# Word loads behind k and v, the first q from another queue, and three steps swapped in the opening of a fused attention and feed-forward kernel

## The chip, the cores and the metric

The kernel runs on one core of one Trainium2 chip. The metric is the device time of one execution in microseconds; three runs of the kernel before took 885.45, 887.29 and 890.8 us, so their median is 887.29 us. Engines are named as the profile names them: PE is TensorE's matmul, PEld its weight load, DVE is VectorE, ACT is ScalarE, POOL is GpSimd, SP is SyncE, which here only starts DMAs.

## The reference

```python
kv  = einsum('bhsd,bhse->bhde', k, v)         # q, k, v: 8 batches, 8 heads, 576 rows, 64 columns, float32
o   = einsum('bhsd,bhde->bhse', q, kv)
x   = o / sqrt(mean(o*o, axis=-1) + 1e-6) * g_norm
x   = x.transpose(0, 2, 1, 3).reshape(4608, 512)
h   = x @ w_in                                # w_in 512 x 2048, w_out 2048 x 512, both float64
out = (h * tanh(softplus(h))) @ w_out         # 4608 x 512, float32
```

The weights arrive as float64. The kernel takes them as pairs of 32-bit words and joins each pair into one float32 number itself.

## The kernel before

The work has two parts. Part 1 goes over nine tiles of 512 tokens. Each tile needs attention's output x, which takes the tile's q and the matrix kv of its batch (or of two batches, since 512 tokens don't divide 576); x is then multiplied by `w_in`, and the activated product g goes to DRAM. Part 2 reads g and multiplies by `w_out`. Both large products are done as two-by-two block products with seven multiplications instead of eight (Strassen's scheme in Winograd's form, `PROD`), and each float32 operand is split into a rounded part and a remainder (`split`, L121 and L122), so that one product is three matmuls.

The opening, with which the change deals, prepares three things at once:

- The eight weight blocks of `w_in` (`conv[0]` to `conv[7]`). A block's steps are LOAD (two DMAs of 512 KB, L137), SCALE (ACT, L142), JOIN (three DVE operations, L147 to L149), DIFF (three DVE operations, L157 to L159), and BLOCKS and SUMS (splits by ACT and DVE). A block's raw words are kept in a room that an earlier block may still hold: blocks 0, 4 and 7 share the tile `w64`, blocks 2 and 5 the tile `wf6`, blocks 3 and 6 the tile `wf7`; block 1 uses `wf5`. A LOAD into a room waits until JOIN of the earlier block has read it.
- k and v. Batch 0's are loaded by `kv_first` (L226) in two halves and multiplied by `kv_first_product` (L234, 72 small matmuls for each half); `kv_keep` (L269) copies the result out of PSUM. For batch 1 the heads go by pairs, p = 0 to 3: `k_load(1, p)` starts four DMAs (L213 and L214, tiles km, kr, vm, vr), `k_product(1, p)` multiplies (L252). Two sets of these tiles exist, so the load of p = 2 waits for the product of p = 0.
- q. The first tile's q comes in four chunks by `rows_load` (L295), each 128 tokens by 8 heads by 64 numbers. TensorE transposes them (step `transpose`, L325: four transposes for each pair of heads; unit 0 takes heads 0 to 3, unit 1 heads 4 to 7), `turned` copies them out of PSUM (ACT for unit 0, L338; DVE for unit 1, L336), `project` multiplies by kv (L360), `square`, `sums`, `rstd` (logarithm L408, exponential L409) and `normalize` (L430) give x.

Every engine works through its instructions in the order in which the code is written. In the opening that order stands in the code directly; from the first product on, `at(t, f)` puts a step behind the product of slot t, and within a slot steps run in the order of the `at` calls. Slot 0 holds the first product (L527), and seven slots make one round.

All DMAs before part 2 are started by SP (its queue is q1 in the profile), but for the stores of the last tile, which ACT starts (queue q10). Each DMA signals one of eight semaphores, which are handed out in turn to the DMAs of SP and ACT together; an instruction that starts a DMA waits until the DMA that had its semaphore before has landed. The order of instructions below writes them DMAHW0 to DMAHW7.

Of the kernel before, what the change touches and what calls it, by code (L numbers as in the profile page):

```python
# [27 lines left out]
def linear_attention_rms_mish_ffn(  # L28
# [34 lines left out]
    nc = tc.nc  # L63
    B, H, S, D = q.shape
# [3 lines left out]
    P = 128  # L68
# [37 lines left out]
    gcol = const.tile([P, 1], F32, name="gcol")  # L106
# [121 lines left out]
    def kv_first_product(n):  # L228
        kt, vt = kv0
        for hp in range(n.start, n.stop):  # L230
            for c in range(9):
                for o in range(2):
                    r, d = slice(o * D, (o + 1) * D), slice(c * D, (c + 1) * D)
                    nc.tensor.matmul(kvps[r, 0, hp, :], kt[r, hp, d], vt[r, hp, d], start=(c == 0), stop=(c == 8))  # L234
# [31 lines left out]
    def kv_keep(b, n):  # L266
        for r in (slice(0, D), slice(D, P)):
            if b < T32:
                nc.scalar.copy(kvf[b][r, n, r], kvps[r, b % 2, n, :])  # L269
        if b < T32 - 1:  # L270
            return
        t = kvt[b % 2]
        for r in (slice(0, D), slice(D, P)):
            nc.scalar.copy(t[r, 0, n, r], kvps[r, b % 2, n, :])
        for r in (slice(0, D), slice(D, P)):
            nc.vector.tensor_sub(t[r, 1, n, r], kvps[r, b % 2, n, :], t[r, 0, n, r].bitcast(F32))


    def segments(j):

        n = (S - T) * j
        segs = []
        if n:
            segs.append((j - 1, S - n, slice(0, n)))
        if n < T:
            segs.append((j, 0, slice(n, T)))
        return segs

    def rows_load(j, c):
        for b, s0, cols in segments(j):  # L290
            t0, t1 = max(cols.start, c * P), min(cols.stop, (c + 1) * P)
            if t0 < t1:
                src = q[b, 0:1, s0 + t0 - cols.start:s0 + t0 - cols.start + 1, :]
                src = bass.AP(src.tensor, src.offset, [[D, t1 - t0], [S * D, H], [1, D]])
                nc.sync.dma_start(rows[j][t0 - c * P:t1 - c * P, c, :].rearrange("p (h d) -> p h d", d=D), src)  # L295

    rows = {}
    qs, ss = {}, {}
# [145 lines left out]
    def x_form(f):  # L444

        a11, a12, a21, a22 = block(0, 0), block(1, 0), block(0, 1), block(1, 1)
        if f == S1:
            nc.vector.tensor_add(xs1, a21, a22)
            nc.vector.tensor_sub(a21, a11, a21)
        elif f == S2:  # L450
            nc.vector.tensor_sub(a11, xs1, a11)  # L451
        elif f == S4:
            nc.vector.tensor_sub(a12, a12, a11)
        if f not in xforms:
            if f == A22:
                xforms[f] = fq.tile([P, 2, 2, TH], F32R, name="a22")
            else:
                pair = {A11: (A11, S1), S2: (S2, A12), S4: (S4, S3)}[f]
                t = fp.tile([P, 2, 2, 2, TH], F32R, name="gf")
                for n, g in enumerate(pair):  # L460
                    xforms[g] = t[:, n]
        t = xforms[f]
        split(t[:, 0], t[:, 1], {A11: a11, S1: xs1, S2: a11, A12: a12, S4: a12, S3: a21, A22: a22}[f])
# [7 lines left out]
    def at(t, f):  # L471
        plan.setdefault(t, []).append(f)
# [86 lines left out]
    def do(j, u, *steps):  # L559
        for s in steps:  # L560
            units[j][u][s]()
# [11 lines left out]
    LOAD, SCALE, JOIN, DIFF, BLOCKS, SUMS, STORE = range(7)  # L573

    def weights(j, *steps):
        for s in steps:
            conv[j][s]()
# [12 lines left out]
    t = wfp.tile([P, 3, 2 * T], F32, name="wf2")  # L590
    rows[0], turned_q = t[:, 0:2].rearrange("p a (c n) -> p (a c) n", c=TR // 2), t[:, 2].rearrange("p (a t) -> p a t", a=2)
    for c in range(TR):
        rows_load(0, c)
    kv0 += [wfp.tile([P, NKC, 9 * D], F32, name=f"wf{n}") for n in (3, 4)]
    kv_first(first)
    weights(1, LOAD)
    kv_first(second)
    for r in (slice(0, D), slice(D, P)):
        nc.sync.dma_start(gcol[r, :], g_norm.rearrange("(p o) -> p o", o=1))
    weights(2, LOAD)  # L600
    weights(4, LOAD)
    weights(3, LOAD)
    make_identity(nc, ident)
    kv_tiles()
# [11 lines left out]
    do(0, 1, "transpose")  # L616
    weights(0, BLOCKS)
    do(0, 0, "turned")
    weights(0, SUMS)
    do(0, 1, "turned")  # L620
    weights(1, SCALE, JOIN)
    kv_first_product(first)
    kv_keep(0, first)
    do(0, 0, "project", "square")
    weights(1, DIFF, BLOCKS)
    kv_first_product(second)
# [6 lines left out]
    k_load(1, 1)  # L633
    rows[1] = att.tile([P, TR, H * D], F32, name="qs")
    for c in range(TR):
        rows_load(1, c)
    do(0, 1, "square", "sums")
    weights(2, SCALE)
    do(0, 0, "normalize")
# [2 lines left out]
    do(0, 1, "rstd", "normalize")  # L642
    x_form(S1)
    weights(2, DIFF)
    weights(5, LOAD)


# [3 lines left out]
    for j in range(3, NF2):  # L651
        t = 3 * (j - 3) + 1
        if j < 5:
            at(t, lambda j=j: weights((6, 7)[j - 3], LOAD))
        for s, n in ((SCALE, 0), (JOIN, 0), (DIFF, 1), (BLOCKS, 1), (SUMS, 2)):
            at(t + n, lambda j=j, s=s: weights(j, s))

# [6 lines left out]
    for b in range(2, B):  # L664
        t = NS * (b - 2)
# [164 lines left out]
    for i in range(NT):  # L830
        for n in range(NQ):
            st = {"i": i, "n": n, "bank": bank_new}
            t = NS * i + 7 * n
# [3 lines left out]
    t = NS * NT  # L837
# [115 lines left out]
```

## Time and profile before

| | |
|---|---|
| three runs, us | 885.45, 887.29, 890.8 (median 887.29) |
| profiled execution, us | 885.97 |
| its span, us | 884.2 |
| PE busy | 828.1 us, 94% of the span |
| DVE busy | 608.7 us, 69% |
| ACT busy | 464.6 us, 53% |
| granted TensorE clock, mean | 0.987 of full speed |

The span runs from the first instruction to the last; the time of the execution is 1.8 us longer. All moments below are microseconds from the span's start. TensorE is nearly always busy, except in the opening: in the page's forty slices of 22 us its busy share is 4, 6 and 5 tenths in the first three, and 8 tenths or more from the fourth to the last but one. In the rows of a timeline the engine, the line and the operation are followed by the tiles (written and read), how many instructions are merged in the row, and in brackets how long the engine was idle before them and what ended that.

### The profile page before, as it was taken

What the parts mean: (1) busy time and instruction counts of PE and PEld (TensorE: products, weight loads), DVE (VectorE), ACT (ScalarE), POOL (GpSimd) and SP (SyncE); (2) the same over time, 40 slices, a digit from 0 to 9 for tenths busy, and PEclk for the clock granted to TensorE, in tenths of its full rate; (3) what the DMA queues carried; (4) which work ended last, traced back from release to release, by engine and by line L of the source; (5) the groups of instructions that cost most, each with busy time, mean ns of one, the idle gap of its engine ahead of it and who ended that gap; (6) DMA issues with size and microseconds to landing.
All of it is one profiled execution on the core that took longest, in us unless ns stands there. A gap on an engine that the chain in (4) does not pass through costs nothing.

```text
span 884.2 us, 17156 instructions
## 1 busy us (share of the span) xinstructions
PE 828.1 (94%) x7036; PEld 795.7 (90%) x7036; DVE 608.7 (69%) x804; ACT 464.6 (53%) x703; POOL 4.8 (1%) x23
## 2 busy tenths in 40 slices
PE   4658998998999999999999899999999999999997
PEld 3447898998999999999999789999999999999997
DVE  5869675886777676787764368867777677776772
ACT  3647666556675765666664444344444434434431
POOL 2000000000000000000000000000000000000000
PEclk9969999999999999999999999999999999999999
DMA  9936787987978696767477993344434443334421
GB/s 294 247 114 197 200 274 246 278 263 226 296 219 278 218 304 199 220 204 227 151 227 249 425 416 125 122 150 152 148 121 133 130 120 120 119 120 141 153 65 48
DMA packets 161038, 175.52 MB, mean 199 GB/s; under 512 B 24704, under 2 KB 142464, under 8 KB 159936
## 3 DMA queue, kind: packets, MB, share of 16 engines
q1 hardware_dynamic: 158208, 170.23, 61.8%
q10 hardware_dynamic: 2752, 4.20, 1.3%
q8 instruction: 55, 0.90, 0.4%
q14 instruction: 23, 0.19, 0.1%
HBM read 112.39 MB, written 62.00 MB: 197 GB/s over the span
## 4 chain that ended last, share of the span: by engine, by line
PE 63%; DMA 11%; DVE 10%; ACT 9%; issue 4%; SPq 2%; ACTq 0%; DVEq 0%
PE a L772 22%; PE bc L772 16%; PE a L527 13%; PE bc L527 7%; DMA gd<-ula 5%; PE s L252 2%; DMA vm<-in_v_dram 2%; DVE ur L548 1%; DMA wod<-wst 1%; ACT L412 1%; ACT gf L121 1%; DMA rd<-fl 1%; DVE gf L122 1%; DVE fa L122 1%; ACT L118 1%
## 5 line engine op out<-in xcount | busy, mean ns | idle before, releaser
L772 PE MATMUL a<-wf,gf 128*128 128x256 f32 x1632 | 201.8, 283 | 0.5 <-DVE ur L812 0.5
L772 PEld LDWEIGHTS a<-wf,gf 128*128 128x128 f32 x1632 | 198.4, 192 | 0.7 <-DVE ur L812 0.7
L122 DVE TENSOR_TENSOR gf<-g,gf 128x1024 fp32r<-128x1024 f32 (+1 forms) x123 | 132.9, 1087 | 90.7 <-ACT gf L121 90.7
L527 PE MATMUL a<-gf,wf 128*128 128x256 f32 x1296 | 173.0, 287 | 11.5 <-DVE gf L430 4.5
L527 PEld LDWEIGHTS a<-gf,wf 128*128 128x128 f32 x1296 | 162.9, 193 | 18.1 <-ACT ur L504 6.6
L527 PE MATMUL bc<-gf,wf 128*128 128x256 f32 x1296 | 170.3, 285 | 3.5 <-ACT ur L495 2.4
L527 PEld LDWEIGHTS bc<-gf,wf 128*128 128x128 f32 x1296 | 161.4, 191 | 5.1 <-ACT ur L495 2.6
L121 ACT CAST gf<-g 128x1024 fp32r<-128x1024 f32 (+1 forms) x123 | 114.6, 939 | 93.3 <-DVE g L752 65.1
L772 PE MATMUL bc<-wf,gf 128*128 128x256 f32 x1224 | 152.7, 283 | 1.0 <-DVE gf L122 1.0
L772 PEld LDWEIGHTS bc<-wf,gf 128*128 128x128 f32 x1224 | 149.4, 192 | 1.4 <-ACT gf L121 0.7
L527 PE MATMUL a<-a,wf 128*128 128x256 f32 x432 | 59.8, 289 | 2.5 <-DVE ur L548 2.5
L527 PEld LDWEIGHTS a<-a,wf 128*128 128x128 f32 x432 | 55.8, 195 | 5.6 <-DVE ur L548 3.1
L118 ACT ACTIVATE ur<-ur 128x1024 f32<-128x1024 f32 x36 | 38.1, 1059 | 37.1 <-DVE ur L548 37.1
L122 DVE TENSOR_TENSOR fa<-fl,fh 128x1024 fp32r<-128x1024 f32 x28 | 34.3, 1224 | 22.1 <-ACT fh L121 21.2
L504 ACT COPY ur<-a 128x512 f32<-128x512 f32 (+1 forms) x53 | 27.3, 516 | 37.6 <-PE a L772 24.6
L122 DVE TENSOR_TENSOR gf<-gf 128x512 fp32r<-128x512 f32 x45 | 30.4, 689 | 24.0 <-ACT gf L121 24.0
L121 ACT CAST gf<-a 128x1024 fp32r<-128x1024 f32 x17 | 17.9, 1052 | 53.5 <-DVE a L749 50.9
L121 ACT CAST gf<-gf 128x512 fp32r<-128x512 f32 x45 | 27.1, 618 | 31.4 <-DVE gf L451 19.1
L495 ACT COPY ur<-bc 128x512 f32<-128x512 f32 (+1 forms) x53 | 27.4, 517 | 29.9 <-PE bc L772 23.0
L548 DVE TENSOR_TENSOR ula<-bc,ula 128x512 f32<-128x512 f32 x36 | 24.8, 688 | 25.4 <-PE bc L527 25.3
L118 ACT ACTIVATE ula<-ula 128x512 f32<-128x512 f32 x36 | 22.8, 633 | 22.1 <-DVE ula L548 22.1
L252 PE MATMUL s<-vm,km 128*64 128x64 f32 x448 | 20.1, 235 | 14.1 <-DMA vm<-in_v_dram 14.1
(137 smaller groups left out, 858.1 us busy)
## 6 DMA issues: line engine op xcount, KB each, us to landing
g<-gd SPq DMA_DIRECT2D x18, 2048.0 KB, 8.9
gd<-ur SPq DMA_DIRECT2D x32, 512.0 KB, 4.0
wod<-wst SPq DMA_DIRECT2D x16, 896.0 KB, 5.6
wf<-wod SPq DMA_DIRECT2D x8, 1792.0 KB, 16.2
gd<-ula SPq DMA_DIRECT2D x32, 256.0 KB, 5.1
gd<-ulb SPq DMA_DIRECT2D x32, 256.0 KB, 4.3
w<-in_moe_w_out_dram SPq DMA_DIRECT2D x32, 256.0 KB, 4.6
km<-in_k_dram SPq DMA_DIRECT2D x28, 256.0 KB, 4.8
```

The source lines that it names most:

```text
L118: nc.scalar.activation(o, i, AF.Mish)
L121: nc.scalar.copy(hi, src)
L122: nc.vector.tensor_sub(lo, src, hi.bitcast(F32))
L252: nc.tensor.matmul(kvps[o * D:(o + 1) * D, b % 2, h0 // 2 + i, :], kt, vt, start=(c == 0), stop=(c == CM))
L412: nc.scalar.preload_act_table_set("natural_log_exp_and_others")
L495: then(t + 2, lambda: nc.scalar.copy(dst(st, "22"), st["c"]))
L504: then(t + 4, lambda: nc.scalar.copy(dst(st, "12"), st["a"]))
L527: nc.tensor.matmul(bank[:, jj], w[:, right, a, kc, :], xf[:, b, kc, :], start=first and jj == kc == s == 0, stop=(kc == 1 and s == 2), ski ...
L548: nc.vector.tensor_add(o, bank, o)
L772: nc.tensor.matmul(bank, gf[:, a, c, :], wo[c][:, right, b, :], start=first and c == s == 0, stop=(c == NF2 - 1 and s == 2), skip_group_ch ...
```

## The change

Four things are moved; nothing is computed in another way.

1. The first tile's q is started by ACT instead of SP (`rows_load` takes the engine as an argument; the second tile's q stays on SP).
2. The two DMAs of `g_norm` are started by GpSimd instead of SP, ahead of its memsets.
3. Block 4's LOAD goes from its place ahead of block 3's to the end of the opening, ahead of block 5's. The LOADs of blocks 6 and 7 go from slots 1 and 4 to slots 3 and 6.
4. In the opening, unit 1's `turned` goes ahead of block 0's SUMS, and block 1's SCALE and JOIN go behind the first `kv_first_product` and `kv_keep`. This is a swap of three steps.

```diff
-    def rows_load(j, c):
+    def rows_load(eng, j, c):
...
-                nc.sync.dma_start(rows[j][t0 - c * P:t1 - c * P, c, :].rearrange("p (h d) -> p h d", d=D), src)
+                eng.dma_start(rows[j][t0 - c * P:t1 - c * P, c, :].rearrange("p (h d) -> p h d", d=D), src)
...
-        rows_load(0, c)
+        rows_load(nc.scalar, 0, c)
...
-        nc.sync.dma_start(gcol[r, :], g_norm.rearrange("(p o) -> p o", o=1))
+        nc.gpsimd.dma_start(gcol[r, :], g_norm.rearrange("(p o) -> p o", o=1))
     weights(2, LOAD)
-    weights(4, LOAD)
     weights(3, LOAD)
...
     do(0, 0, "turned")
+    do(0, 1, "turned")
     weights(0, SUMS)
-    do(0, 1, "turned")
-    weights(1, SCALE, JOIN)
     kv_first_product(first)
     kv_keep(0, first)
+    weights(1, SCALE, JOIN)
     do(0, 0, "project", "square")
...
-        rows_load(1, c)
+        rows_load(nc.sync, 1, c)
...
     weights(2, DIFF)
+    weights(4, LOAD)
     weights(5, LOAD)
...
-            at(t, lambda j=j: weights((6, 7)[j - 3], LOAD))
+            at(t + 2, lambda j=j: weights((6, 7)[j - 3], LOAD))
```

Where the instructions stand shows at three places. The first is ACT's beginning. Before, its first rows are these (w is block 0's words, the tile wf that L142 reads is block 1's words, the tiles x and s are in PSUM):

```order
L588 ACT_TABLE_LOAD
L142 ACTIVATE fl<-w_136 128x1024
L121 CAST wf_217<-fl 128x256
L121 CAST wf_217<-fl 128x2x256
L338 COPY fh<-x_198 128x1024
L121 CAST wf_217<-wd 128x4x256
L142 ACTIVATE fl<-wf_148 128x1024
L269 COPY kvf_168<-s_123 64x2x64 x2
L370 ACTIVATE fa<-x_271 128x1024
```

With the change they are these:

```order
L588 ACT_TABLE_LOAD
L295 DMA wf_139<-in_q_dram 128x8x64 x4
L142 ACTIVATE fl<-w_136 128x1024
L121 CAST wf_214<-fl 128x256
L121 CAST wf_214<-fl 128x2x256
L338 COPY fh<-x_195 128x1024
L121 CAST wf_214<-wd 128x4x256
L269 COPY kvf_165<-s_123 64x2x64 x2
L142 ACTIVATE fl<-wf_148 128x1024
L370 ACTIVATE fa<-x_268 128x1024
```

The four q DMAs stand ahead of ACT's first scale, and the copies of kv stand ahead of block 1's scale instead of behind it.

The second place is SP's beginning with the change, with what each start waits for (w_136, wf_148, wf_155 and wf_158 are the words of blocks 0, 1, 2 and 3; wf_144 and wf_145 are batch 0's k and v). The four q chunks hold the semaphores DMAHW1, 3, 5 and 7:

```order
L137 DMA w_136<-in_moe_w_in_dram 128x4x256 x2
L226 DMA wf_144<-in_k_dram 128x2x576
L226 DMA wf_145<-in_v_dram 128x2x576
L137 DMA wf_148<-in_moe_w_in_dram 128x4x256 [waits DMAHW0_49]
L137 DMA wf_148<-in_moe_w_in_dram 128x4x256 [waits DMAHW1_49]
L226 DMA wf_144<-in_k_dram 128x2x576 [waits DMAHW2_49]
L226 DMA wf_145<-in_v_dram 128x2x576 [waits DMAHW3_49]
L137 DMA wf_155<-in_moe_w_in_dram 128x4x256 [waits DMAHW4_49]
L137 DMA wf_155<-in_moe_w_in_dram 128x4x256 [waits DMAHW5_49]
L137 DMA wf_158<-in_moe_w_in_dram 128x4x256 [waits DMAHW6_49]
L137 DMA wf_158<-in_moe_w_in_dram 128x4x256 [waits DMAHW7_49]
```

The q DMAs, which stood between block 0's words and k, are gone from SP; the second halves of blocks 1 and 2 and the second v now wait for a chunk of q that ACT has started.

The third place is SP around the second tile's q (qs) and the third quarter of batch 1's k and v (km to vr). Before (wf_387 is block 5, wf_441 block 6):

```order
L295 DMA qs<-in_q_dram 128x8x64 x3
L137 DMA wf_387<-in_moe_w_in_dram 128x4x256 x2
L137 DMA wf_441<-in_moe_w_in_dram 128x4x256 x2
L213 DMA km<-in_k_dram 128x2x256
L214 DMA kr<-in_k_dram 64x2x64
L213 DMA vm<-in_v_dram 128x2x256
L214 DMA vr<-in_v_dram 64x2x64
```

With the change (w_384 is block 4, wf_387 block 5, wf_522 block 6; the four rows of the fourth quarter are left out):

```order
L295 DMA qs<-in_q_dram 128x8x64 x3
L137 DMA w_384<-in_moe_w_in_dram 128x4x256 x2
L137 DMA wf_387<-in_moe_w_in_dram 128x4x256 x2
L213 DMA km<-in_k_dram 128x2x256
L214 DMA kr<-in_k_dram 64x2x64
L213 DMA vm<-in_v_dram 128x2x256
L214 DMA vr<-in_v_dram 64x2x64
...
L137 DMA wf_522<-in_moe_w_in_dram 128x4x256 x2
```

Block 6's words have gone behind two quarters of k and v, and block 4's words have come in ahead of block 5's. TensorE's order is the same in both kernels.

## Rows read from the trace of the kernel before

**Rows 1.** Stages: us, busy PE, PEld, DVE, ACT, POOL, clock, DMA share, GB/s.
```profile
0.00:7.50 7.50, 0.00 (x0) 0.00 (x0) 0.00 (x1) 2.40 (x2) 4.76 (x23) 1.00 0.84 210
7.50:14.30 6.80, 4.43 (x16) 3.18 (x16) 5.62 (x8) 2.88 (x4) 0.00 (x0) 1.00 1.17 311
14.30:20.00 5.70, 3.44 (x75) 2.89 (x76) 3.92 (x5) 1.53 (x4) 0.00 (x0) 1.00 1.06 358
...
54.60:57.00 2.40, 2.38 (x24) 2.17 (x25) 0.00 (x0) 0.00 (x0) 0.00 (x0) 0.50 0.32 78
...
72.00:90.00 18.00, 18.00 (x142) 14.73 (x141) 16.21 (x22) 12.18 (x17) 0.00 (x0) 0.91 0.52 163
```

**Rows 2.** SP's longest wait (total, times, longest), then timeline: start, us, engine, line.
```profile
SPq L137 <- DVE fl L149: 20.8, 2, 11.0
...
35.19 12.57 SPq L137 DMA_DIRECT2D wf<-in_moe_w_in_dram  x4
...
37.52 0.48 PE L252 MATMUL s<-vr,kr 64*64 64x64 f32 x4
...
47.86 0.45 SPq L213 DMA_DIRECT2D km<-in_k_dram  x1
...
54.62 1.12 PE L252 MATMUL s<-vm,km 128*64 128x64 f32 x16 [12.88 <-DMA vm<-in_v_dram]
```

**Rows 3.** Timeline, 50 to 72 us: ACT and DVE around TensorE's wait.
```profile
50.31 1.04 ACT L121 CAST wf<-wd 128x1024 fp32r<-128x1024 f32 x1
...
51.73 1.22 DVE L122 TENSOR_TENSOR wf<-wd,wf 128x1024 fp32r<-128x1024 f32 x1
...
59.05 0.58 ACT L504 COPY ur<-a 128x512 f32<-128x512 f32 x1 [7.70 <-PE a L527]
59.53 1.12 ACT L142 ACTIVATE fl<-w 128x1024 f32<-128x1024 f32 x1
...
60.69 0.69 DVE L147 TENSOR_SCALAR fl<-fl 128x1024 uint32<-128x1024 uint32 x1 [7.74 <-ACT fl L142]
...
71.75 1.22 PE L325 MATMUL x<-ident,qs 128*128 128x128 f32 x8 [2.54 <-ACT gf L378]
```

**Rows 4.** Timeline, 1 to 25 us: the opening.
```profile
1.79 5.30 SPq L295 DMA_DIRECT2D wf<-in_q_dram  x4
...
10.99 1.33 PE L325 MATMUL x<-ident,wf 128*128 128x128 f32 x5 [0.60 <-DMA wf<-in_q_dram]
...
12.11 1.91 PE L325 MATMUL a<-ident,wf 128*128 128x128 f32 x8
...
14.35 2.39 PE L234 MATMUL s<-wf,wf 64*64 64x64 f32 x72 [0.32 <-DMA wf<-in_v_dram]
...
17.32 1.12 ACT L142 ACTIVATE fl<-wf 128x1024 f32<-128x1024 f32 x1 [3.01 <-DMA wf<-in_moe_w_in_dram]
18.34 0.51 ACT L269 COPY kvf<-s 64x128 f32<-64x128 f32 x2
18.47 0.69 DVE L147 TENSOR_SCALAR fl<-fl 128x1024 uint32<-128x1024 uint32 x1 [1.71 <-ACT fl L142]
...
20.46 1.22 DVE L149 SCALAR_TENSOR_TENSOR fl<-wf,fl 128x1024 uint32<-128x1024 uint32 x1
...
22.90 0.42 DVE L159 TENSOR_TENSOR wd<-fl,wd 128x256 f32<-128x256 f32 x1
...
23.75 1.05 ACT L121 CAST wf<-wd 128x1024 fp32r<-128x1024 f32 x1
...
24.82 1.27 ACT L408 ACTIVATE fa<-bc,eps 128x512 f32<-128x512 f32 x2
```

**Rows 5.** DMA queues (packets, MB, share), first 5 to 10, then 490 to 498 us.
```profile
q1 hardware_dynamic: 4219, 1.17, 135.2%
...
q1 hardware_dynamic: 247, 3.11, 91.3%
q10 hardware_dynamic: 247, 0.25, 9.0%
```

## The prediction

> **What bounds the kernel now.** I read the stages first, then the instructions in order of time of the two stretches in which TensorE stands, then the DMA queues. From 72 us on TensorE is busy without a gap: 18.00 of 18.00 us in the stage from 72 to 90 [rows 1]. So the change, which touches only the beginning, can win or lose only what it does to the moment at which TensorE enters that stage, and everything behind it is carried along by the same number of microseconds. Ahead of it stands the largest single wait of the program. SP starts a group of four word loads at 35.19 us that takes 12.57 us, nearly all of it a wait (11.0 us) for VectorE's L149, the join of block 3 [rows 2]. The first two of the four load block 5; the last two load block 6 into the room that the join of block 3 has to free. Behind them, in order, sit the k and v of batch 1's third quarter: km is issued at 47.86 us, and TensorE, which has waited 12.88 us, goes on at 54.62 us [rows 2].
>
> That wait isn't worth its length, because TensorE isn't the slowest engine of this stretch. VectorE works through normalization, x forms and the weight blocks 2 and 3 until 52.95 us (51.73 + 1.22), ScalarE's last cast for block 3 ends at 51.35 us (50.31 + 1.04) [rows 3]. Only then, in ScalarE's order, come the copy L504 and the scale of block 4, and only behind that scale VectorE's join of block 4. Here they stood at 59.05, 59.53 and 60.69 us because L504 waited 7.70 us for TensorE [rows 3]. Take TensorE's wait away wholly, and L504 begins at 51.35 us, its 0.58 and the scale's 1.12 us follow, and the join begins at about 53.1 us: 60.69 - 53.1 = 7.6 us earlier. TensorE's next wait, 2.54 us at 71.75 us, ends with ScalarE's chain behind this join [rows 3], so the 7.6 us are handed on. They are the most that the moved loads can give, as long as VectorE's chain starts when it does now.
>
> **The moved loads.** Block 4's load goes behind batch 1's first k, v and the second tile's q, block 6's behind the third and fourth quarters of k and v, block 7's one quarter further. All bytes are as before. The price: block 6's words come later by the issue of eight k and v DMAs. They are wanted only behind the joins and differences of blocks 4 and 5, some 4.8 us of VectorE each by block 1's rows [rows 4], and 1 MB takes about 3 us at 358 GB/s [rows 1]; that is the cover, and I cost it at nothing. If it were too short, the join of block 6 would wait, and only for the remainder. What stays ahead of the third quarter's k and v is block 5's load, which waits for the join of block 2, long before the point where the k and v rooms come free. So the stall goes, worth 7.6 us, and late next is VectorE's chain itself: whatever shifts its start, shifts the end.
>
> **q from ScalarE's queue.** On SP the four q DMAs take 5.30 us of issue [rows 4]. Without them k, v are issued at 1.79 instead of about 7.1 us. But the issue isn't what the beginning waits for: it is the transfer. From 7.5 to 20 us the DMA engines carry 311 and 358 GB/s [rows 1], and the same engines must bring the same bytes. What changes is the order in which they do it. Now q stands between block 0's words and k, v, alone at the head of its queue, and moves 4219 packets in 5 us [rows 5], nearly all of them q's rows of 64 floats. In the change, two queues are open at once. The trace has such a place: from 490 to 498 us each queue moves 247 packets, the one 3.11 MB and the other 0.25 MB [rows 5]. The turn is one packet each, whatever the size. q has 4 x 1024 packets of 256 bytes. Against them SP has block 0 (1024 packets of 1 KB), k, v (512), block 1 (1024), k, v (512), block 2 (1024): 4096, the same number. So the last q chunk is served when nearly all of block 2 is.
>
> The Trainium skill has the same order of service, in "DMA: Bandwidth & Descriptors", section "Queues, rings and completion order": an engine goes round its queues packet by packet. Its section "Issuing engines are not separate DMA queues" says that starting DMAs from several engines saves only the sequencer's issue time. By the second rule alone q would cost nothing and the 5.30 us of issue would be the bound of a gain; by the first it costs the delay worked out below. The trace agrees with the first (247 against 247).
>
> When is that? Block 0 to 2 are 3 x 1.049 MB, q 1.049, k and v 2.36, together 6.55 MB. The kernel before had moved 7.5 x 210 + 6.8 x 311 + 5.7 x 358 KB = 5.73 MB by 20 us [rows 1]; the last 0.82 MB at 358 GB/s take 2.3 us more: 22.3 us. The second half of block 2 has to wait for the third q chunk before SP may issue it (the semaphores of the DMAs are eight, used in turn), which could take its 0.52 MB out: 20.8 us; the packet's way to the semaphore adds something again. I take 22.3 us for the landing of the last q, between 20.8 and about 24, against 10.98 us now [rows 4].
>
> **From q to VectorE's chain.** Call this landing Q. TensorE then does five transposes (1.33 us), eight more (1.91) and the 72 k, v products (2.39) [rows 4]; v's first half has long landed. The swapped step lets ScalarE keep the result at once (0.51) instead of behind block 1's scale, which waited 3.01 us for its words; the scale (1.12) now comes behind. Then VectorE joins block 1 (from 18.47 to 21.68 now: 3.21 us), forms its differences (to 23.32: 1.64), ScalarE casts them (1.05) and takes the logarithm, which stood at 24.82 us [rows 4]. Added up: 1.33 + 1.91 + 2.39 + 0.51 + 1.12 + 3.21 + 1.64 + 1.05 = 13.16 us, with the overlaps of ends and starts about 13.1. The logarithm starts at Q + 13.1 = 35.4 us, 10.6 us later than now. From there to the end of VectorE's block 3 nothing waits for TensorE or a load, so the whole chain moves by 10.6 us, and the join of block 4 goes from 53.1 to 63.7 us: 3.0 us later than 60.69. In a formula: change = Q - 19.3.
>
> The other swapped step (VectorE's two copies ahead of block 0's sums) only puts one subtraction behind two copies, before a scale that VectorE waits for anyway: nothing. g_norm's two tiny DMAs go to GpSimd ahead of its 4.76 us of memsets [rows 1]; the zeroed tiles are wanted behind Q: nothing, and even at the end of those memsets, 2 us before the 7.5 us at which TensorE begins now, two short issues have room. ScalarE is held by q's issue; even if that lasted until 11 us, its work and VectorE's on block 0 would end before Q.
>
> **Sum.** -7.6 + 10.6 = +3.0 us. The profiled execution took 885.97 us (span 884.2): 888.97. It lies 1.3 us under the median of the three runs, 887.29, which spread over 5.4 us; I write 889.
>
> **Rivals.**
> *q is served in time.* If packets of 256 bytes get more turns, or SP's queue runs dry while it waits for semaphores, Q stays at 11 to 14 us. At 11 the start is earlier by 0.7 us and the stall's 7.6 us remain: 885.97 - 8.3 = 877.7; at 14 us 880.7. For it: SP may hold only eight unfinished DMAs, q's included, so block 1's second half waits for q's first chunk. Against: its queue already holds 1536 packets by then, and the 247 to 247. Faster by over 0.5% (which is about what a measurement of this kernel can tell from no change) begins at Q = 14.9.
> *TensorE comes back slow.* After its wait of 12.8 us TensorE was granted 0.50, 1.2 instead of 2.4 GHz, from 54.6 to 57 us [rows 1]. In the change it stands, but for a few transposes, until Q. The transposes and products of the sum, 5.6 us, would take up to as much again: 889 + 5.6 = 894.6 at most, 892 for half of it. Slower by over 0.5% is reached when 1.5 us of this come true, or Q passes 23.8 us. Against: up to 20 us the clock is 1.00 now, although TensorE is idle for the first 7.5 us [rows 1].
> *The order of the k, v loads binds instead.* Third-quarter k, v are issued when the first quarter's product ends, now at 38.0 us (37.52 + 0.48), then 10.6 us later at 48.6; with the 6.8 us from issue to use that this load has now (47.86 to 54.62) they are there at 55.4, 0.8 us later than now [rows 2]. VectorE's 3.0 us is the later one still. Only for a load that took 2.2 us more would this bind.
>
> **Chances.** q late and clock full, 887 to 891.5: 0.46. q in time: 0.30, all of it faster. Slow clock or a still later q: 0.24, nearly all slower. So faster 0.30, same 0.45, slower 0.25. The time is that of the first, 889; the range for eight in ten reaches from 878 to 893.5.
>
> **What would show it.** The last q transposes of the first unit at 21 to 24 us, the 72 products right behind, the first product of the feed-forward 10 us later than now; no wait of TensorE for vm above 6 us; VectorE without a gap of more than 1.5 us from normalization to the join of block 4 at 63 to 65 us. If the q chunks land by 14 us, the queue rule is where I was wrong; if the join comes as worked out and the end doesn't follow, the stages behind 72 us have slack that I don't see.

## Result and profile after

The changed kernel is slower by half a per cent: a median of 891.86 us over 13 runs against 887.08 us over 13 runs of the kernel before on the same chips, ratio 1.0049 with a 95% interval of 1.0033 to 1.0065, which is 2.9 to 5.8 us. Its profiled execution took 889.18 us with a span of 887.4 us, 3.2 us above the one of before (885.97 and 884.2).

The opening first, in order of time (start, duration, engine, line, then what the engine waited for), against [rows 4]:

```profile
0.78 9.47 ACTq L295 DMA_DIRECT2D wf<-in_q_dram  x4
...
10.36 1.12 ACT L142 ACTIVATE fl<-w 128x1024 f32<-128x1024 f32 x1 [8.32 <-issue]
...
14.16 0.47 PE L325 MATMUL x<-ident,wf 128*128 128x128 f32 x1 [7.28 <-DMA wf<-in_q_dram]
...
19.15 0.47 PE L325 MATMUL x<-ident,wf 128*128 128x128 f32 x1 [4.51 <-DMA wf<-in_q_dram]
...
23.16 1.33 PE L325 MATMUL x<-ident,wf 128*128 128x128 f32 x5 [3.54 <-DMA wf<-in_q_dram]
...
25.38 0.69 DVE L336 COPY wf<-a 128x512 f32<-128x512 f32 x1 [8.08 <-PE a L325]
...
26.13 2.50 PE L234 MATMUL s<-wf,wf 64*64 64x64 f32 x72
...
28.73 0.53 ACT L269 COPY kvf<-s 64x128 f32<-64x128 f32 x2 [2.25 <-PE s L234]
...
30.47 0.69 DVE L147 TENSOR_SCALAR fl<-fl 128x1024 uint32<-128x1024 uint32 x1 [2.41 <-ACT fl L142]
...
36.43 1.27 ACT L408 ACTIVATE fa<-bc,eps 128x512 f32<-128x512 f32 x2
```

ACT needs 9.47 us to start the four q DMAs, and the last three chunks are used at 14.16, 19.15 and 23.16 us; in the kernel before, the last was used at 10.99 us. Everything that hangs on it follows, down to the logarithm at 36.43 instead of 24.82 us.

Next the place where TensorE stood for 12.88 us [rows 2], and where ScalarE and VectorE go on to block 4 [rows 3]:

```profile
54.99 0.69 PE L252 MATMUL s<-vm,km 128*64 128x64 f32 x16 [1.10 <-DMA vm<-in_v_dram]
...
62.88 0.58 ACT L504 COPY ur<-a 128x512 f32<-128x512 f32 x1
63.36 1.15 ACT L142 ACTIVATE fl<-w 128x1024 f32<-128x1024 f32 x1
...
64.54 0.69 DVE L147 TENSOR_SCALAR fl<-fl 128x1024 uint32<-128x1024 uint32 x1
...
75.62 1.09 PE L325 MATMUL x<-ident,qs 128*128 128x128 f32 x8 [1.44 <-ACT gf L378]
```

The wait for vm is down to 1.10 us, so the moved loads do what they are for. But L504 and the join of block 4 no longer wait for TensorE (neither row has a bracket); they come 3.8 us later than before because the whole chain ahead of them started 11.6 us later. TensorE enters its dense stretch at 75.62 instead of 71.75 us, and behind it there is no gap, as before [rows 1]:

```profile
76.00:90.00 14.00, 14.00 (x110) 11.32 (x109) 12.30 (x18) 8.97 (x15) 0.00 (x0) 1.00 0.50 147
```

How the two queues were served while both had work shows in 3 us of the opening, from 11 to 14 us (packets, MB, share), against the second group of [rows 5]:

```profile
q1 hardware_dynamic: 729, 0.77, 84.0%
q10 hardware_dynamic: 726, 0.18, 28.3%
```

One packet each, with four times the bytes for the queue with the larger packets. From 9 to 16 us the counts stay as equal (1478 and 1480); from 3 to 7 us they weren't (890 of SP's, 1154 of q's), and from 16 to 18 us, when SP's queue had run low, q moved 969 beside 181.

### The profile page after: what moved, and what is told of

The parts are those of the page before. It is cut to its first block, busy times and chain, and to the rows that moved or that the text cites. A ratio compares the mean times of both kernels' runs of the same rounds, so it can differ in the third digit from the quotient of the medians.

```text
span 887.4 us, 17159 instructions
## 1 busy us (share of the span) xinstructions
PE 829.7 (93%) x7036; PEld 795.7 (90%) x7036; DVE 608.8 (69%) x804; ACT 464.8 (52%) x703; POOL 6.0 (1%) x25
## 4 chain that ended last, share of the span: by engine, by line
PE 63%; DVE 11%; DMA 11%; ACT 10%; issue 4%; SPq 1%; ACTq 0%; DVEq 0%
PE a L772 21%; PE bc L772 16%; PE a L527 13%; PE bc L527 8%; DMA gd<-ula 5%; DMA wf<-in_q_dram 2%; PE s L252 2%; DMA vm<-in_v_dram 1%; DVE ur L548 1%; ACT L412 1%; DVE fl L148 1%; DMA rd<-fl 1%; DVE gf L122 1%; ACT L118 1%; DVE fl L149 1%
## 5 line engine op out<-in xcount | busy, mean ns | idle before, releaser
L527 PE MATMUL a<-gf,wf 128*128 128x256 f32 x1296 | 173.7, 288 | 10.6 <-ACT ur L504 4.1
L504 ACT COPY ur<-a 128x512 f32<-128x512 f32 (+1 forms) x53 | 27.3, 516 | 30.2 <-PE a L772 24.6
L548 DVE TENSOR_TENSOR ur<-bc,ur 128x512 f32<-128x512 f32 x36 | 24.4, 678 | 10.3 <-ACT ur L504 6.2
```

The costliest lines, as they stand in the source:

```text
L504: then(t + 4, lambda: nc.scalar.copy(dst(st, "12"), st["a"]))
L527: nc.tensor.matmul(bank[:, jj], w[:, right, a, kc, :], xf[:, b, kc, :], start=first and jj == kc == s == 0, stop=(kc == 1 and s == 2), ski ...
L548: nc.vector.tensor_add(o, bank, o)
```

## Experiments

Theory A is the prediction's: the late q costs about 11 us, the moved loads give about 7.5, the swapped steps nearly nothing. Each run is compared with runs of the kernel before on the same chip.

**q back on SP.**

```diff
-        rows_load(nc.scalar, 0, c)
+        rows_load(nc.sync, 0, c)
```

> The changed kernel with only the first tile's q started by SP again, between block 0's words and k. Theory A (q is served late because two open queues take turns packet by packet, and this eats the gain of the moved loads): the last q chunk is used at 11 to 12 us instead of 23.2, the join of block 4 begins at 52 to 53 us instead of 64.5, the time is about 8 us under the kernel before, a ratio of 0.990 to 0.992. Rival B (the late word blocks make VectorE wait, so the moved loads bring nothing): ratio 0.998 or more, with the join of block 4 at 60 us or later.

Measured: 879.68 us, ratio 0.9932 (0.9912 to 0.9952). The last chunk and the join of block 4:

```profile
11.23 1.33 PE L325 MATMUL x<-ident,wf 128*128 128x128 f32 x5 [0.42 <-DMA wf<-in_q_dram]
...
53.20 0.69 DVE L147 TENSOR_SCALAR fl<-fl 128x1024 uint32<-128x1024 uint32 x1
```

One argument turns the slower kernel into a faster one, which ends rival B. The join is where it was expected within half a microsecond; the gain of about 6 us stops short of the 8 expected, and the interval just reaches the expected range.

**q on ACT's queue alone**, in the kernel before.

> The kernel before with only the first tile's q started by ACT. Theory A: the last q chunk is used at 22 to 24 us, everything from there on moves by about 10 us, and the wait for vm stays above 10 us, since block 6's load still stands ahead of it and waits for a join that has moved too: ratio 1.010 to 1.013. Rival C (the 12.9 us wait of TensorE swallows a late start): ratio at most 1.003, and the wait for vm is down to 3 us or less.

Measured: 893.66 us, ratio 1.0095 (1.0074 to 1.0116), 8.4 us. The ratio lies just below the range that was expected, and its interval reaches into it. What SP, TensorE and VectorE do:

```profile
13.23 0.48 PE L325 MATMUL x<-ident,wf 128*128 128x128 f32 x1 [6.15 <-DMA wf<-in_q_dram]
...
13.61 4.94 SPq L599 DMA_DIRECT2D gcol<-in_g_norm_dram  x2
...
18.10 0.47 PE L325 MATMUL x<-ident,wf 128*128 128x128 f32 x1 [4.39 <-DMA wf<-in_q_dram]
...
20.42 1.33 PE L325 MATMUL x<-ident,wf 128*128 128x128 f32 x5 [1.84 <-DMA wf<-in_q_dram]
...
23.38 3.51 PE L234 MATMUL s<-wf,wf 64*64 64x64 f32 x72
...
62.83 1.12 PE L252 MATMUL s<-vm,km 128*64 128x64 f32 x16 [12.32 <-DMA vm<-in_v_dram]
...
68.87 0.69 DVE L147 TENSOR_SCALAR fl<-fl 128x1024 uint32<-128x1024 uint32 x1 [7.23 <-ACT fl L142]
```

The wait for vm isn't swallowed: it is 12.32 us long again and has only moved. Rival C falls. q arrives at 20.42 us, 2.7 us sooner than in the changed kernel. Here g_norm still goes through SP, and its two starts held SP for 4.94 us, until 18.55 us, so block 2's words, which in the changed kernel SP begins to start at 14.55 us, came behind. That fits the last chunk, which follows the third by 2.32 us here and by 4.01 us there. About 1 us of the lead was there before: the second chunk is used at 13.23 us here and at 14.16 us there, and why stays open. g_norm's move wasn't run alone, so its part isn't shown.

**The moved loads alone**, in the kernel before.

```diff
     weights(2, LOAD)
-    weights(4, LOAD)
     weights(3, LOAD)
...
+    weights(4, LOAD)
     weights(5, LOAD)
...
-            at(t, lambda j=j: weights((6, 7)[j - 3], LOAD))
+            at(t + 2, lambda j=j: weights((6, 7)[j - 3], LOAD))
```

> The kernel before with only the LOADs of blocks 4, 6 and 7 moved. Theory A: no wait for vm above 2 us, the join of block 4 at about 53.1 us instead of 60.7, ratio 0.9905 to 0.9925 (7.6 us). Rival B (late blocks make VectorE wait): ratio 0.998 or more.

Measured: 878.51 us, ratio 0.9917 (0.9900 to 0.9934), 7.4 us, where 7.6 were worked out. This version is faster than both kernels. The wait for vm was expected to go below 2 us; it went to 4.41:

```profile
45.88 1.12 PE L252 MATMUL s<-vm,km 128*64 128x64 f32 x16 [4.41 <-DMA vm<-in_v_dram]
...
51.05 0.58 ACT L504 COPY ur<-a 128x512 f32<-128x512 f32 x1
...
52.71 0.69 DVE L147 TENSOR_SCALAR fl<-fl 128x1024 uint32<-128x1024 uint32 x1
```

L504 begins without a wait all the same, so the remaining 4.41 us cost nothing that shows: ScalarE was not ready earlier.

**The three swapped steps alone**, in the kernel before.

> The kernel before with only the three steps swapped. Theory A: the projection starts 1.5 us earlier, but block 1's join now follows ScalarE's later scale, so the first logarithm comes only 0.5 us earlier or at the same moment: ratio 0.999 to 1.000. Rival D (the swap lengthens VectorE's chain and is part of what made the changed kernel slower): ratio 1.001 or more, the first logarithm later than 25 us.

Measured: 885.68 us, ratio 0.9996 (0.9984 to 1.0007): no difference that can be measured. The projection starts at 17.65 instead of 18.95 us, the logarithm at 24.71 instead of 24.82 us:

```profile
17.65 1.95 PE L360 MATMUL x<-fh,kvf 128*128 128x512 f32 x4 [0.72 <-issue]
...
24.71 1.26 ACT L408 ACTIVATE fa<-bc,eps 128x512 f32<-128x512 f32 x2
```

The 1.3 us aren't passed on: ahead of the logarithm stands the cast of block 1, whose join now starts 0.28 us later (18.75 us). Rival D is not seen in this kernel.

**SP held back until q has landed**, in the changed kernel.

```diff
     kv_first(first)
+    gate = tc.dram_tile([1, D], F32, name="gate")
+    nc.sync.dma_start(gate, rows[0][0:1, TR - 1, 0:D])
     weights(1, LOAD)
```

> The changed kernel, q on ACT's queue as there, with one more tiny DMA on SP behind batch 0's first k, v: it stores 256 bytes of the last q chunk to DRAM, so SP starts block 1's words and all that follows only once q has landed. Theory A (turns of one packet between the two queues): q's 4096 packets then meet only 1536 of SP's, the last chunk is used at 13 to 15 us instead of 23.2, the first logarithm starts 13 us behind it, and the time is 4 to 6 us under the kernel before: ratio 0.993 to 0.9965. Rival E (q is slow on ACT's queue by itself, by its start or its 256-byte rows): the last chunk stays at 20 us or later, ratio 1.000 or more.

Measured: 883.89 us, ratio 0.9975 (0.9962 to 0.9988), a gain of 2.2 us over the kernel before and about 6.5 over the changed one. The queues from 2 to 14 us, and the opening:

```profile
q1 hardware_dynamic: 1578, 2.21, 54.8%
q10 hardware_dynamic: 4052, 1.02, 42.9%
```

```profile
15.14 1.33 PE L325 MATMUL x<-ident,wf 128*128 128x128 f32 x5 [0.39 <-DMA wf<-in_q_dram]
...
18.10 3.33 PE L234 MATMUL s<-wf,wf 64*64 64x64 f32 x72
...
25.19 2.31 PE L234 MATMUL s<-wf,wf 64*64 64x64 f32 x72 [1.06 <-DMA wf<-in_v_dram]
...
29.23 1.27 ACT L408 ACTIVATE fa<-bc,eps 128x512 f32<-128x512 f32 x2
```

With q on the same queue, started by the same engine, but without company after its first third, the last chunk comes 8.0 us earlier. That ends rival E: q isn't slow on ACT's queue by itself, it is slowed by what SP has open beside it. Beside the 1536 packets that SP still starts before the gate, it came 3.9 us later than from SP's own queue (11.23 us). The ratio misses the range that was expected by 0.001, about 1 us, and its interval reaches into it. The last chunk came a little late (15.14, against 13 to 15), the first 72 products took 3.33 us instead of 2.4 at a granted clock of 1.00, which I can't explain (with q alone they took 3.51), and the second half waited for v, which the gate had delayed.

**VectorE given about 3 us more**, on top of the moved loads alone; the result is unchanged. `times` is 3 for block 2 and 1 for the others.

```diff
-            nc.vector.tensor_sub(d[:, 0:2], x[:, 2:4], x[:, 0:4:2])
...
+            for _ in range(times):
+                nc.vector.tensor_sub(d[:, 0:2], x[:, 2:4], x[:, 0:4:2])
...
```

> The kernel before with only the loads moved (as in the run e3_loads_alone), and block 2's three difference operations on VectorE done three times over instead of once, with the same result: 3.3 us more of VectorE between the first and the second product. Theory A' (with the wait for vm gone, VectorE's chain from normalization to the join of block 4 sets the end): the whole 3.3 us arrive, the join of block 4 at 56 us instead of 52.7, ratio 0.994 to 0.997 (0.9917 without the addition). Rival F (TensorE's loads of k and v bind, VectorE has slack): at most 1 us arrives, ratio at most 0.993.

Measured: 883.58 us, ratio 0.9964 (0.9950 to 0.9977). Without the addition it was 0.9917, so 0.0047 or 4.2 us arrive. In the trace each repetition takes 1.52 us, so 3.04 us were added, not 3.3; the logarithm starts 0.73 us later than with the moved loads alone (25.34 and 24.61). Both arrive in full: the join of block 4 and TensorE's entry into the dense stretch come 3.81 us later (with the moved loads alone 52.71 and 63.76). The 4.2 us are the same within the two intervals:

```profile
56.52 0.69 DVE L147 TENSOR_SCALAR fl<-fl 128x1024 uint32<-128x1024 uint32 x1
...
67.57 1.97 PE L326 MATMUL x<-ident,qs 128*128 128x128 f32 x8 [4.11 <-ACT gf L379]
```

VectorE's chain is what sets the end once the wait for vm is gone. Rival F falls.

**Block 1's scale ahead of the k, v product again**, in the changed kernel.

```diff
+    weights(1, SCALE, JOIN)
     kv_first_product(first)
     kv_keep(0, first)
-    weights(1, SCALE, JOIN)
```

> The changed kernel with block 1's scale and join back ahead of the first k, v product and its copy. Theory A: with q as late as 23 us, block 1's words are there long before, so the scale and the join run while TensorE waits for q, and the first logarithm comes 1 us or more earlier than in the changed kernel (36.4 us): 34.8 to 35.5 us; the time falls by about 1 us. Rival D' (the swap is worth its 1.5 us in this kernel too): the logarithm at 37 us or later.

One run, 887.82 us, no interval. The last chunk came at 22.59 us (23.16 in the changed kernel); the join of block 1 starts 3.07 us earlier than there and the logarithm 1.96 us, a little more than was expected:

```profile
22.59 1.33 PE L325 MATMUL x<-ident,wf 128*128 128x128 f32 x5 [3.06 <-DMA wf<-in_q_dram]
...
25.55 2.31 PE L234 MATMUL s<-wf,wf 64*64 64x64 f32 x72
...
27.40 0.69 DVE L147 TENSOR_SCALAR fl<-fl 128x1024 uint32<-128x1024 uint32 x1
...
34.47 1.27 ACT L408 ACTIVATE fa<-bc,eps 128x512 f32<-128x512 f32 x2
```

Of the 1.96 us, 0.57 are the earlier q; up to 1.4 us are the order (0.19 of them lie in the first 72 products, 2.31 us instead of 2.50). So the swap, worth nothing in the kernel before, costs something once q is late. Rival D' falls in the trace; the time of a single run doesn't decide it.

**GpSimd instead of VectorE for the differences**, on top of the moved loads alone: an attempt at a better version.

```diff
-            nc.vector.tensor_sub(d[:, 0:2], x[:, 2:4], x[:, 0:4:2])
...
+            (nc.vector if put or j == 0 else nc.gpsimd).tensor_sub(d[:, 0:2], x[:, 2:4], x[:, 0:4:2])
...
```

The other two difference operations are changed in the same way; block 0 and the blocks of `w_out` (`put`) stay on VectorE.

> The kernel before with only the loads moved, and the three difference operations of blocks 1 to 7 done by GpSimd instead of VectorE, with the same result: a version that could beat both kernels. Theory A' (VectorE's chain sets the end of the opening): VectorE loses 1.6 us of work for each of the blocks 1, 2 and 3 ahead of the join of block 4, so this join begins 1 to 3 us earlier than in e3_loads_alone (52.7 us), until TensorE's own path binds: ratio 0.9875 to 0.9905. Rival G (GpSimd takes longer for the operations than VectorE, and the casts wait for it): join of block 4 at 53 us or later, ratio 0.992 or more.

Measured: 883.25 us, ratio 0.9971 (0.9962 to 0.9981), slower than the moved loads alone by 0.0054. The largest difference operation on GpSimd (count, busy us, mean ns, idle time before it) and the join of block 4:

```profile
L157 POOL TENSOR_TENSOR wd<-fl 128x512 f32<-128x512 f32 x7 | 9.3, 1329 | 60.2 <-DVE fl L149 60.2
```

```profile
53.90 0.69 DVE L147 TENSOR_SCALAR fl<-fl 128x1024 uint32<-128x1024 uint32 x1 [0.31 <-ACT fl L142]
```

Rival G holds: the operation takes 1329 ns instead of 690, and the join comes 1.2 us later instead of earlier. TensorE's entry comes 1.1 us later (64.90 and 63.76). This explains 1.1 of the 4.8 us; the rest is lost behind the entry, where GpSimd still does the differences of blocks 5 to 7, and was not followed up. The best version stays the moved loads alone.

**All of them in one table.** The start of the first logarithm (L408), the entry, which is the moment at which TensorE starts the second tile's second set of transposes (the row at 71.75 us in [rows 3]), the time between them, the span, and what lies between the entry and its end:

| run | logarithm, us | entry, us | between, us | span, us | from entry to end, us |
|---|---|---|---|---|---|
| before | 24.82 | 71.75 | 46.93 | 884.2 | 812.5 |
| changed | 36.43 | 75.62 | 39.19 | 887.4 | 811.8 |
| q back on SP | 25.08 | 64.24 | 39.16 | 878.0 | 813.8 |
| q on ACT alone | 33.51 | 79.93 | 46.42 | 891.6 | 811.7 |
| moved loads alone | 24.61 | 63.76 | 39.15 | 876.1 | 812.3 |
| swapped steps alone | 24.71 | 71.30 | 46.59 | 883.7 | 812.4 |
| SP held back | 29.23 | 68.42 | 39.19 | 882.0 | 813.6 |
| VectorE given more | 25.34 | 67.57 | 42.23 | 879.9 | 812.3 |
| scale first | 34.47 | 73.64 | 39.17 | 886.0 | 812.4 |
| GpSimd's differences | 26.13 | 64.90 | 38.77 | 882.1 | 817.2 |

In the first nine runs the entry differs by over 16 us, and what lies behind it stays within 2.1 us; the last one changes work behind the entry too. The way from the logarithm to the entry takes 39.15 to 39.19 us in all five kernels that have the moved loads and nothing else changed on that way, whether q comes early or late, and 46.4 to 46.9 us in the three without them.

## Why the prediction was right

It said 889 us, in a range from 878 to 893.5, by a sum of -7.6 and +10.6, with a change of under half a per cent as the likeliest outcome (0.45). Measured are 891.86 us and +2.9 to +5.8, in the profiled executions +3.2; the entry, which the sum works out, came 3.87 us later, where +3.0 was forecast. The loss is half a per cent, at the very edge of that outcome, and its interval excludes no change. The median lies 0.36 us above the 887 to 891.5 us of its main case. Of the 2.86 us above 889, 1.1 come from adding the sum to the profiled execution, which lies that much under the median of the 13 runs, and 0.9 from q, which landed later than taken; the rest isn't settled.

1. *The entry carries everything behind it.* Shown by the first nine rows of the table above.
2. *The stall is worth 7.6 us, not 12.9.* Shown: the moved loads alone give 7.4 us, the join of block 4 begins at 52.71 us (53.1 was worked out), L504 without a wait, and what is added to VectorE's chain arrives in full. The way from logarithm to entry is 7.7 us shorter in the changed kernel than before. TensorE's own idle time was the wrong number to read there; the right one was the idle time of the engine that comes next in the chain.
3. *q is served packet by packet against SP's loads, and lands at 22.3 us.* It landed at 23.16 us. That turns are taken shows in 729 against 726 packets; that SP's loads beside it are the cause, in the run with SP held back. The working was too even, though: in the 5 us from 18 to 23.1 us q moved only its last 260 packets, beside 1425 of SP's:

```profile
q1 hardware_dynamic: 1425, 1.70, 101.0%
q10 hardware_dynamic: 260, 0.06, 6.4%
```

Most of q had come by 18 us, when SP's queue had run low for a moment, and a rest took 5 us more. So it is in part luck that the number came within 0.9 us: by 18 us q had moved 3900 packets and SP's queue 2955, so q was ahead of the even turns, and a slow rest, which the working didn't have, took the lead away again. A rest on a few of the sixteen DMA engines, each of which keeps taking turns, would fit. In the run with SP held back, where q ends without company, the busy share of the sixteen engines falls step by step over more than a microsecond (tenths, forty slices from 11 to 15 us):

```profile
DMA  9999999999999999999999976444333221100000
```

That fits too, but the traces don't say which engine carried which packet, so it is not shown.

4. *From the last q to the logarithm 13.1 us.* Right: 36.43 - 23.16 = 13.27.
5. *VectorE's chain moves by as much, the join of block 4 comes 3.0 us later.* The logarithm came 11.6 us later (10.6 forecast, nearly all of the difference is q's landing), the join 3.85, the entry 3.87.
6. *The swapped steps give nothing.* Right in the kernel before (0.9996). In the changed kernel the sum took the swapped order as given and did not ask what the old one would have been worth: up to 1.4 us by the scale-first run. By itself q on ACT costs 8.4 us, the loads give 7.4 and the steps 0.4; together that would be +0.6 us, not +4.3. Of the 3.7 us between, 2.9 show in the logarithm, which starts at 36.43 us in the changed kernel and at 33.51 with q alone, and 2.7 of these are q's earlier landing there. The order's 1.4 us can't be added to that: with q alone the old order took 13.09 us from the last q to the logarithm, nearly the 13.27 of the new one, with 72 products of 3.51 us on the way (in the scale-first run 11.88 us, with products of 2.31). The remaining 0.8 us are within the intervals of the ratios.
7. *Third-quarter k, v in place at 55.4 us.* They were used at 54.99 us, but by two misses that cancel: km was issued at 49.87 us instead of 48.6, and from issue to use it took 5.1 us instead of 6.8.
8. *ScalarE held by the q DMAs until 11 us at no cost.* Right: it was free at 10.36 us, and VectorE stood idle for 8.08 us, until 25.38 us, all the same.
9. The rivals: q in time didn't come, and the run with q back on SP shows what it would have been worth (about 6 us). The slow clock didn't come where it was feared: 1.00, the 2.4 GHz level, was granted until 23.1 us, although TensorE had been busy for 1.40 us only, and to 37 us, over all products of the sum. It fell to 0.50 later, from 42 to 49 us, and there the way from the logarithm to the entry is as long as in the other kernels with the moved loads.

```profile
0.00:23.10 23.10, 1.40 (x3) 0.55 (x3) 5.62 (x8) 3.33 (x4) 5.97 (x25) 1.00 0.97 289
23.10:37.00 13.90, 13.10 (x169) 9.28 (x169) 8.70 (x12) 7.61 (x12) 0.00 (x0) 1.00 0.95 249
...
42.00:49.00 7.00, 3.41 (x19) 2.93 (x20) 6.86 (x10) 2.36 (x3) 0.00 (x0) 0.50 0.37 118
```

Not settled: why the medians lie 4.8 us apart and the two profiled executions 3.2. The interval of the ratio holds both.

## What to carry to other kernels

A transfer that the start of a kernel waits for belongs on the queue where its place in the order is sure; on a second queue it shares turns with everything that the first has open. Small packets lose by that: here those of 256 bytes moved 0.18 MB while as many of SP's moved 0.77. A wait of the busiest engine is worth only what the next slowest chain leaves of it: look how long the engines behind it have been idle at its end. Of a bundle of edits each is worth a run of its own: here one part gave 7.4 us, another cost 8.4, and the whole was a small loss; the parts run alone did not add up to it either.

## What the runs showed of the hardware

- Two hardware queues moved equal numbers of packets with loads from DRAM on both sides too, mostly of 1024 bytes against 256 (729 and 726 packets in 3 us, 1478 and 1480 in 7 us); the trace of before showed it for a load beside a store. In the first microseconds and at the end of the transfer the numbers weren't equal (890 and 1154 from 3 to 7 us, 1425 and 260 from 18 to 23.1 us).
- The last packets of a transfer took long: q's last 260 of 4096 took 5 us beside SP's loads, and with nothing beside them the engines' busy share fell from 9 tenths to none over 1.3 us (SP held back).
- Starting four DMAs of 1024 packets each kept ACT for 9.47 us beside SP's loads, and its first scale began at 10.36 us; on SP it took 5.30 us [rows 4].
- A 128 x 512 float32 subtraction took 1329 ns on GpSimd, and 690 ns on VectorE.
